# Pooled attention into a sine MLP: batch 1's q turned on VectorE, and one more inner product per unit

## The chip, the cores and the metric

The kernel runs on one core of a Trainium2 chip. Its time is device time in microseconds (us) of one launch; the kernel before has a median of 899.21 us over 3 runs (898.9 to 899.62). The profile is one execution taken by the hardware profiler; its span leaves out what lies around the program's work, so it is a little shorter than the time of a run. The engines are TensorE (PE in the profile; PEld is its weight load), VectorE (DVE), ScalarE (ACT), GpSimd (POOL) and SyncE (SP), which issues most of the DMAs.

## The reference

```python
# q, k, v: (8 batches, 8 heads, 576 rows, 64), float32
k_p = k.reshape(B, H, 72, 8, D).mean(axis=3)
v_p = v.reshape(B, H, 72, 8, D).mean(axis=3)
scores = scale * np.matmul(q, k_p.transpose(0, 1, 3, 2))
scores = scores - np.max(scores, axis=-1, keepdims=True)
attn = np.exp(scores)
attn = attn / (np.sum(attn, axis=-1, keepdims=True) + 1e-09)
out = np.matmul(attn, v_p)                       # then x: (4608 tokens, 512)
h = x @ w_in                                     # w_in: 512 x 2048
s = np.sin(alpha * h)
g = h + s * s / (alpha + 1e-09)
return g @ w_out                                 # w_out: 2048 x 512
```

Keys and values are averaged over runs of 8 rows, so each query sees only 72 of them.

## The kernel before

Everything is float32. The attention of one batch gives 576 tokens; the first matmul of the MLP goes over the 4608 tokens in 9 *units* of 512. Units 0 to 8 fill the first 517 us or so; then comes the second matmul (line L1383) to the end.

**A unit.** The first matmul is cut in halves three ways (features of x, columns of w_in, tokens) and done as seven products in place of eight, from sums of blocks (a Strassen-Winograd scheme). `hidden` runs a unit as 4 groups J of 7 *slots*, so 28 slots a unit. A slot has about one product of the group: 4 matmuls of 128x256, each recorded as 2 instructions (line L866). A group's products go to four PSUM banks `b1`, `b6`, `b5`, `b7`; ScalarE copies one bank into another so that a product adds onto it (L839), `p5` is ScalarE's copy of the fifth product to SBUF, VectorE adds `p5` to banks (L838), ScalarE takes sines (L1028) and squares (L1035), VectorE adds the squares (L1080, one add of 128x512 from PSUM and one of 128x1024 from SBUF per group) in `finish`, and `store_g` sends the result to DRAM. The tail of a group's work runs beside the first slots of the next: in the code `Q` is the group before and `G` the present one.

**The inner form.** `inner_product` does one product again as seven smaller ones: 7 matmuls of 128x128 (L1058) in place of 4 of 128x256, in four pieces `a`, `b`, `d`, `e`, between which ScalarE makes three copies (L1062, L1064, L1068) and VectorE one add (L1073). It needs sums of blocks of w_in, which GpSimd makes once in `inner_w_in` (L823), and of x, made per unit in `inner_x`. For units 1 to 6 the fifth product of groups 2 and 3 and the first of group 3 have this form (`I5 = (2, 3)`, `I1 = (3,)`).

**The attention beside it.** `carry(u)` hangs the attention of batch u + 1 on the slots of unit u by hand: a list of calls per slot, issued in that order to each engine's queue. For one batch: `load_k` and `load_v` bring k and v to SBUF, GpSimd pools them (L132), TensorE turns the pooled k (`k_t`, L279) and makes the scores in two halves (`two_scores`, L318), VectorE takes maxima and differences (`two_shifts`, L341 and L342), ScalarE the exponentials (`exp`, L367), VectorE sums and reciprocals (`norm`, L373 and L374), GpSimd multiplies (L375), VectorE turns 32x32 blocks (`turn`, L504), DMAs move them (`move`) and TensorE makes the outputs (`all_values`). Sine and exponential use different function tables of ScalarE, so a group of exps has a table load ahead of it and the next sine has another.

**q, in two ways.** The scores need q with its 64 features along the partitions. For batches 2 to 7 `turn_q` does that in two steps: VectorE transposes 32x32 blocks (L229 twice, L234 once) into `tr`, and 16 DMAs on SP's queue (L244) put the blocks in place. For batches 0 and 1 TensorE does it: for batch 1, `pairs_q` makes ScalarE put the heads in pairs (5 copies, L98), `q_t` makes 20 transposes on TensorE (L290) into PSUM in 5 steps, and each step has a copy back to SBUF (L291, two on VectorE, three on ScalarE). `columns` gives the layout of the scores' operand, which differs between the two ways.

**Queues.** Each engine runs its own list in order. DMAs issued on SP go out in order, about 0.6 us for each issue of q's moves, over eight semaphores taken in turn, so an issue waits for the one eight before it.

Of the kernel before, what the change touches and what calls it, by code (L numbers as in the profile page):

```python
# [19 lines left out]
P = 128  # L20
# [20 lines left out]
class Kernel:  # L41
# [46 lines left out]
    def pairs_q(self, b, tiles):  # L88

        nc = self.nc  # L90
        if 0 in tiles:
            self.raw = self.q_views(self.qm[b])
            self.qm[b] = self.q_tile(1)
        x = self.qm[b][:].rearrange("p (t h e d) -> p t e h d", t=5, e=2, d=self.D)
        for t in tiles:
            n = P if t < 4 else 64
            raw = self.raw[0][:, :, t, :] if t < 4 else self.raw[1]
            nc.scalar.copy(out=x[:n, t], in_=raw.rearrange("p (e h) d -> p e h d", e=2))  # L98

    def load_q_rest(self, b, at=None):  # L100
        if b < 2:
            self.nc.sync.dma_start(out=self.q_views(self.qm[b])[1] if at is None else at, in_=self.q[b, :, 4 * P:, :].rearrange("h p d -> p h d"))
# [31 lines left out]
    def load_v(self, b):  # L134

        nc, D, H = self.nc, self.D, self.H
        vm, vz = self.vp[b] = self.ap.tile([P, H // 2, D], F32, name="vm", bufs=2), self.ap.tile([P, H // 2, D], F32, name="vz", bufs=2)
        t = self.kvp.tile([P, 2048], F32, name="kvin")[:].rearrange("p (h x) -> p h x", h=4)
        x = self.kvp.tile([P, POOL * D], F32, name="vr", bufs=1)[:]
        for s in range(2):  # L140
            nc.sync.dma_start(out=t[64 * s:64 * s + 64],
                              in_=self.v[b, 4 * s:4 * s + 4, 0:4 * P, :].rearrange("h (p t) d -> p h (t d)", t=POOL))
# [5 lines left out]
        self.pool_rows(t, vm[:])  # L148
# [66 lines left out]

    def turn_q(self, b, part):
# [42 lines left out]
    def attention(self, b):  # L259
# [22 lines left out]
        def q_t(i, copy=nc.scalar.copy):  # L282

            n = rows[i]
            x = self.qm[b][:n].rearrange("p (t hp x) -> p t hp x", t=5, hp=NP)[:, i]
            if b not in self.qt:
                self.qt[b] = self.qt_view(self.q_tile(0))
            ps = self.abank([P, NP, P])
            for hp in range(NP):
                nc.tensor.transpose(ps[:, hp, :n], x[:, hp], self.ident[:n, :n])  # L290
            copy(out=self.qt_tiles(b)[:, i, :, :n], in_=ps[:, :, :n])  # L291

        def columns(hp, i):

            if b < 2:
# [230 lines left out]
        def to_x(ps, hp, t0, m, s0=0):  # L526

            while s0 < m:
# [5 lines left out]
                if t0 and b > 1:  # L534
# [8 lines left out]
        def value_parts(hp, rest):  # L543
# [14 lines left out]
            order = lambda x: x.rearrange("p a (t i) -> p t a i", i=32) if b == 1 else x  # L558
            at = lambda r, n, h: order(self.aM[r:r + n, :, 128 * h:128 * h + 128])
# [74 lines left out]
        return SimpleNamespace(**{f.__name__: f for f in (k_t, q_t, products, score, two_scores, two_shifts, exp, norm, new_a, turn, move, values, values_rest, all_values,  # L634
# [200 lines left out]
    def hidden(self, u, extra):  # L835
# [41 lines left out]
        for slot in range(7 * self.NJ):  # L877
# [9 lines left out]
            if k == 0:  # L887
# [4 lines left out]
                if G.i5 and not N:  # L892
                    G.i5.a()
                if Q and not G.i5 and not end(J):
# [5 lines left out]
                else:  # L900
                    product(G, 1, G.b1, True)
                    if G.i5:
                        product(Q, 4, Q.b7, part=(2, 3))
            elif k == 1:
                if not G.i1:
                    copy(G.b6[:], G.b1[:])
                if G.i5 and not G.i1:
# [9 lines left out]
            elif k == 2:  # L917
                if Q and not G.i5 and not split(J):
                    self.finish(Q)
                if not G.i1:  # L920
                    extras()
                if G.i1:
# [16 lines left out]
            elif k == 3:  # L939
                late = J == 0 and busy  # L940
                if Q and not late and not G.i5 and not split(J):
# [11 lines left out]
                else:  # L953
                    copy(G.b7[:], G.b6[:])
                    if G.i5:
# [10 lines left out]
                    product(G, 2, G.b1)  # L966
            elif k == 4:
# [5 lines left out]
                if not G.i5:  # L973
# [6 lines left out]
                if G.i5:  # L980
# [19 lines left out]
            else:  # L1000
# [3 lines left out]
                sin(G, 1, 1, G.g[:, 1, :, 1])  # L1004
# [19 lines left out]
    def sin(self, G, i, j, src):  # L1024

        for jj in range(JW):
# [78 lines left out]
    def first_batch(self):  # L1105
# [88 lines left out]
        self.load_w_in_part(0, ((2, 1, 0),))  # L1194
        for e in range(2):
            self.load_k(1, e)
            self.pool_k[e]()
        self.combine_w_in(0, (3,), nc.gpsimd)
# [3 lines left out]
    def carry(self, u):  # L1202
# [6 lines left out]
        if u == 0:  # L1209
# [7 lines left out]
            at(2, self.sums_of_x, 0, 3)  # L1217
# [9 lines left out]
            at(7, lambda: self.pool_v())  # L1227
# [3 lines left out]
            for i in range(2, 5):  # L1231
                at((8, 8, 9)[i - 2], A.q_t, i)
            at(9, A0.exp, 4)
            at(13, A0.norm_rest)
# [4 lines left out]
            at(8, self.combine_w_in, 2, (0, 1, 2, 3), self.nc.gpsimd)  # L1239
            at(17, self.combine_w_in, 3, (0, 1), self.nc.gpsimd)  # L1240
            at(17, self.combine_w_in, 3, (2, 3), self.nc.gpsimd)
            at(21, A0.a_rest)
            at(24.5, lambda: A0.values_rest((5, 6, 7, (self.turn + 1) % 5)))
            for r in (32, 96):
                at(3, self.nc.gpsimd.memset, self.aM[r:r + 32, :, 704:736], 0.0)
# [3 lines left out]
            at(9, self.load_q, 2)  # L1249
            at(23, lambda: self.inner_w_in(((5, 2, 4), (1, 3, 4)), (lambda w: [w[:, i * 2 * P:i * 2 * P + 2 * P] for i in range(8)])(self.q_tile(0))))  # L1250
# [3 lines left out]
            at(27, self.att[2].k_t)  # L1254
            turn = 23
# [3 lines left out]
        if 0 < u < last:  # L1259
# [453 lines left out]
```

## Time and profile before

| what | value |
|---|---|
| median of 3 runs | 899.21 us (898.9 to 899.62) |
| span of the profiled execution | 896.2 us |
| matmuls of the inner form, L1058, one group | 72 records, mean 275 ns |
| L866, 128x256, the largest group | 1072 records, mean 381 ns |
| ScalarE's exps, L367 | 29, 19.8 us |
| table loads of ScalarE at L367 and L1028 | 8 and 9, 1283 ns each |
| GpSimd's multiplies of the exps, L375 | 28, mean 1270 ns |
| DMA queue of the hardware, q1 | 137.39 MB, 52.6% of 16 engines' span |

Lines of the profile name the code line, the engine, the operation, output and input, and a count; then the busy time with the mean of one, and the idle time ahead of them. In a timeline the first number is the start in us from the span's start, the second the time that the run of like instructions takes. TensorE's matmuls overlap, so the distance from one start to the next says what one costs.

### The profile page before, as it was taken

What the parts mean: (1) busy time and instruction counts of PE and PEld (TensorE: products, weight loads), DVE (VectorE), ACT (ScalarE), POOL (GpSimd) and SP (SyncE); (2) the same over time, 40 slices, a digit from 0 to 9 for tenths busy, and PEclk for the clock granted to TensorE, in tenths of its full rate; (3) what the DMA queues carried; (4) which work ended last, traced back from release to release, by engine and by line L of the source; (5) the groups of instructions that cost most, each with busy time, mean ns of one, the idle gap of its engine ahead of it and who ended that gap; (6) DMA issues with size and microseconds to landing.
All of it is one profiled execution on the core that took longest, in us unless ns stands there. A gap on an engine that the chain in (4) does not pass through costs nothing.

```text
span 896.2 us, 16276 instructions
## 1 busy us (share of the span) xinstructions
PE 890.8 (99%) x6274; PEld 813.9 (91%) x6274; DVE 682.9 (76%) x918; ACT 438.6 (49%) x1033; POOL 249.2 (28%) x265
## 2 busy tenths in 40 slices
PE   9999999999999999999999999999999999999998
PEld 6787888888888888888888999999999999999998
DVE  7786857768577675765677889898897896996885
ACT  6687776877768777687776711111111211111111
POOL 6798443825338252434523000000000000000000
PEclk9999999999999999999999999999999999999999
DMA  9857957759586585648126243716435355164002
GB/s 269 244 158 206 244 147 212 187 164 254 139 214 186 183 225 147 175 140 302 53 106 219 102 181 103 232 37 218 117 105 160 89 159 159 37 192 142 20 18 53
DMA packets 119533, 141.03 MB, mean 157 GB/s; under 512 B 45776, under 2 KB 86496, under 8 KB 119456
## 3 DMA queue, kind: packets, MB, share of 16 engines
q1 hardware_dynamic: 116288, 137.39, 52.6%
q10 hardware_dynamic: 3168, 2.61, 1.0%
q8 instruction: 50, 0.82, 0.4%
q14 instruction: 27, 0.22, 0.1%
HBM read 75.37 MB, written 47.19 MB: 137 GB/s over the span
## 4 chain that ended last, share of the span: by engine, by line
PE 99%; DVE 0%; POOL 0%; ACT 0%; issue 0%; DVEq 0%
PE PS L866 44%; PE PS L1383 43%; PE PS L1058 5%; PE PS L318 2%; PE PS L613 2%; PE PS L626 1%; PE PS L1126 0%; PE PS L571 0%; PE PS L290 0%; PE PS L425 0%; PE PS L279 0%; PE PS L479 0%; PE PS L569 0%; POOL tr L451 0%; PE PS L403 0%; PE PS L487 0%
## 5 line engine op out<-in xcount | busy, mean ns | idle before, releaser
L866 PE MATMUL PS<-home,a 128*128 128x256 f32 x1072 | 253.0, 381 | 0.1
L866 PEld LDWEIGHTS PS<-home,a 128*128 128x128 f32 x1072 | 198.4, 190 | 30.9 <-issue 4.6
L866 PE MATMUL PS<-home,as 128*128 128x256 f32 x736 | 177.2, 382 | 0.0
L866 PEld LDWEIGHTS PS<-home,as 128*128 128x128 f32 x736 | 134.5, 190 | 18.1 <-ACT PS L839 1.2
L1383 PE MATMUL PS<-s,wb 128*128 128x192 f32 x672 | 116.2, 326 | 0.0
L1035 ACT ACTIVATE s<-s,c 128x256 f32<-128x256 f32 (+1 forms) x236 | 115.5, 556 | 0.0
L1383 PEld LDWEIGHTS PS<-s,wb 128*128 128x128 f32 x672 | 110.4, 190 | 0.1
L132 POOL TENSOR_TENSOR kvin<-kvin 96x768 f32<-96x768 f32 (+3 forms) x42 | 73.4, 1747 | 69.9 <-DMA kvin<-in_v_dram 67.8
L838 DVE TENSOR_TENSOR h<-PS,p 128x512 f32<-128x512 f32 x72 | 49.2, 684 | 55.5 <-PE PS L866 35.2
L1554 ACT COPY PS<-PS 128x192 f32<-128x192 f32 x42 | 12.7, 303 | 146.2 <-PE PS L1383 130.0
L1028 ACT ACTIVATE s<-h,al 128x256 f32<-128x256 f32 x144 | 65.5, 509 | 32.6 <-DVE h L838 32.6
L1383 PE MATMUL PS<-r,wb 128*128 128x192 f32 x432 | 79.0, 326 | 0.0
L1383 PEld LDWEIGHTS PS<-r,wb 128*128 128x128 f32 x432 | 71.6, 190 | 0.0
L1383 PE MATMUL PS<-s,a 128*128 128x192 f32 x384 | 70.2, 326 | 0.0
L1028 ACT ACTIVATE s<-PS,al 128x256 f32<-128x256 f32 x144 | 60.0, 469 | 17.2 <-PE PS L866 16.5
L1383 PEld LDWEIGHTS PS<-s,a 128*128 128x128 f32 x384 | 63.7, 190 | 0.0
L1080 DVE TENSOR_TENSOR h<-PS,s 128x512 f32<-128x512 f32 x36 | 24.8, 689 | 48.6 <-ACT s L1035 48.6
L839 ACT COPY PS<-PS 128x512 f32<-128x512 f32 x72 | 41.5, 577 | 34.5 <-PE PS L866 26.7
L1080 DVE TENSOR_TENSOR h<-h,s 128x1024 f32<-128x1024 f32 x36 | 55.3, 1537 | 3.3 <-ACT s L1035 3.1
L1584 ACT COPY PS<-PS 128x192 f32<-128x192 f32 x42 | 12.7, 303 | 89.5 <-PE PS L1383 89.5
L1322 DVE TENSOR_TENSOR s<-r 128x768 f32<-128x768 f32 x54 | 51.4, 951 | 4.8 <-PE PS L1383 2.8
L1383 PE MATMUL PS<-s,we 128*128 128x192 f32 x288 | 52.7, 326 | 0.0
(244 smaller groups left out, 1401.4 us busy)
## 6 DMA issues: line engine op xcount, KB each, us to landing
g_bridge<-h SPq DMA_DIRECT2D x72, 512.0 KB
r<-g_bridge SPq DMA_DIRECT2D x15, 1536.0 KB
x<-g_bridge SPq DMA_DIRECT2D x8, 1536.0 KB
out_dram<-o SPq DMA_DIRECT2D x90, 96.0 KB
kvin<-in_k_dram SPq DMA_DIRECT2D x14, 576.0 KB
q<-in_q_dram SPq DMA_DIRECT2D x7, 1024.0 KB
kvin<-in_v_dram SPq DMA_DIRECT2D x14, 512.0 KB
aM<-tr SPq DMA_DIRECT2D x54, 92.0 KB
```

The lines of the kernel that those rows point to most:

```text
L132: self.nc.gpsimd.tensor_tensor(out=t[..., 0:w] if w > D else out, in0=t[..., 0:w], in1=t[..., w:2 * w], op=OP.add)
L318: nc.tensor.matmul(ps[e][r0 + r:r0 + r + q.shape[-1], h, :], q[s], kb[s, hp, :], start=True, stop=True)
L613: nc.tensor.matmul(o[r:r + 64], w, x, start=start and i < 2, stop=False, skip_group_check=True)
L838: add = lambda o, x, y: nc.vector.tensor_tensor(out=o, in0=x, in1=y, op=OP.add)
L839: copy = lambda o, x: nc.scalar.copy(out=o, in_=x)
L866: nc.tensor.matmul(ps[:, jj, :], self.A[p][:, kk, f * P:(f + 1) * P], x[:, kk, :], start=(start and n == 0), stop=(kk == 1), skip_group_ch ...
L1028: self.nc.scalar.activation(out=G.s[:, i, jj, j, :], in_=src[:, jj], func=AF.Sin, scale=self.al[:, f:f + 1])
L1035: self.nc.scalar.activation(out=x, in_=x, func=AF.Square, scale=self.c[:, f:f + 1])
L1058: nc.tensor.matmul(o, W[m][:, G.J - J0], X[m], start=start and n == 0, stop=True, skip_group_check=True)
L1080: add = lambda o, x, y: self.nc.vector.tensor_tensor(out=o, in0=x, in1=y, op=OP.add)
L1322: tt = lambda o, x, y, op: nc.vector.tensor_tensor(out=o, in0=x, in1=y, op=op)
L1383: nc.tensor.matmul(out, W[:, J // 2, J % 2, :], A[:, J, :], start=(start and J == 0), stop=(J == self.NJ - 1), skip_group_check=True)
```

## The change

1. Batch 1's q is loaded raw and turned as that of batches 2 to 7 are: `pairs_q` and `q_t` go; `turn_first_q` makes three VectorE transposes and 16 DMAs on SP's queue. The last 64 rows of q are loaded in two DMAs where one did before. The batch then has the same layout as the later ones.
2. `load_v` is cut in parts: the two DMAs of the main halves, and the rest. GpSimd's pooling of the main part is a call of its own.
3. In unit 0 the work of batch 1 is hung on other slots: the moves of q stand in SP's queue with the main halves of v and w_in's part 3 between and behind them; the score halves go from slots 6 and 11 to 10 and 12; k's turn from slot 4 to 6; exps, norms and turns follow. GpSimd's sums of w_in stand at slots 4, 6, 10.5 and 16, and, ahead of unit 0, those of part 0 stand before k's pooling.
4. In units 1 to 6 the fifth product of group 1 takes the inner form too. The group's slots are re-ordered (`fast`): two halves of products are put a slot later or cut to make room, the copy `p5` comes behind the exps of slot 10, and the group's last sine goes to the next group. GpSimd's sums for the inner form are 128x384 wide in place of 128x256.
5. In these units the exps go in two pairs, at slots 6 and 10 in place of 8, 9, 10 and 10, with a one-element sine (`sine_table`) behind the first pair, so that the sine table is loaded there. Norms go to slots 7, 7, 10, 12 and turns to 9, 13, 13, 13. The main halves of v for the batch after are loaded at slot 21 of the unit before, pooled at slot 5; the rest of v stays at slot 6 (loads) and 12 (pooling).

```diff
+    def turn_first_q(self, part):
+        nc = self.nc
+        if part == 0:
+            self.tr = self.new_tr()
+            self.qt[1] = self.q_tile(1)[:]
+        tr = self.tr[:, 0:2560].rearrange("p (k x) -> p k x", k=2)
+        if part < 2:
+            x = self.q_views(self.qm[1])[0][:, 4 * part:4 * part + 4].rearrange("p hp t (k i) -> p (hp t) k i", i=32)
+            nc.vector.transpose(out=tr[:, :, 768 * part:768 * part + 512].rearrange("p k (n i) -> p n k i", i=32), in_=x)
+            return
...
+        for e, a in (((0, 1), (0, 2), (0, 3)), ((1, 0), (0, 0), (1, 1)), ((1, 2), (1, 3)))[part - 3]:
+            w = 768 if a == e else 512
+            to, at = (512, 512) if a == e == 1 else (self.q_at(a), 768 * e)
+            for k in range(2):
+                r = 64 * e + 32 * k
+                nc.sync.dma_start(out=self.qt[1][r:r + 32, to:to + w], in_=tr[32 * a:32 * a + 32, k, at:at + w])
...
-        I5, I1 = ((2, 3), (3,)) if busy else {7: ((2, 3), (2, 3)), 8: ((2, 3), (2, 3))}.get(u, ((), ()))
+        I5, I1 = ((1, 2, 3), (3,)) if busy else {7: ((2, 3), (2, 3)), 8: ((2, 3), (2, 3))}.get(u, ((), ()))
+        fast = lambda G: busy and G.J == 1
...
+                if fast(G):
+                    sin(Q, 0, 1, Q.g[:, 0, :, 1], (1,))
+                    G.i5.b()
+                    square(Q, 0, 1)
+                    product(Q, 4, Q.b7, part=(2, 3))
+                    self.last_sines(Q, 1)
+                    squares(Q, 1)
...
+                if fast(G):
+                    product(G, 6, G.b6, part=(0, 1))
+                    G.i5.d()
+                    self.finish(Q)
...
+                    if fast(G):
+                        product(G, 2, G.b1, part=(0, 1))
+                        G.i5.e()
...
                     extras()
-                    product(G, 2, G.b1)
+                    if fast(G):
+                        copy(G.p5[:], G.b5[:])
+                    product(G, 2, G.b1, part=(2, 3) if fast(G) else range(4))
...
-                sin(G, 1, 1, G.g[:, 1, :, 1])
+                if not fast(G):
+                    sin(G, 1, 1, G.g[:, 1, :, 1])
...
+    def sine_table(self):
+        self.nc.scalar.activation(out=self.sm.tile([P, 1], F32, name="order")[:], in_=self.al[:, 0:1], func=AF.Sin)
...
             for i in range(4):
-                at((8, 9, 10, 10)[i], A.exp, i)
-                at((9, 10, 11, 12)[i], A.norm, i)
-                at((12, 13, 13, 13)[i], A.turn, i)
+                at((6,6,10,10)[i], A.exp, i)
+                at((7,7,10,12)[i], A.norm, i)
+            for i in range(4):
+                at((9,13,13,13)[i], A.turn, i)
+            at(6, self.sine_table)
             at(14, A.move, range(4))
-            at(6, self.load_v, b)
+            at(5, lambda: self.pool_v_main())
+            if b < last:
+                at(21, self.load_v, b + 1, (0, 1))
+            at(6, self.load_v, b, (2,))
             at(12, lambda: self.pool_v())
```

Unit 0's list in `carry`, as far as batch 1's q, k, v and scores go:

```diff
-            at(2, self.load_w_in_part, 3)
-            at(2, self.pairs_q, 1, (0, 1))
-            at(3, self.pairs_q, 1, (2, 3, 4))
-            at(4, A.q_t, 0, self.nc.vector.tensor_copy)
-            at(4, A.q_t, 1, self.nc.vector.tensor_copy)
-            at(4, A.k_t)
-            at(7, self.load_v, 1)
+            at(3, self.turn_first_q, 0)
+            at(3, self.turn_first_q, 3)
+            for part in (1, 2, 4):
+                at(5, self.turn_first_q, part)
+            at(5, self.load_v, 1, (0,))
+            at(5, self.turn_first_q, 5)
+            at(5, self.load_v, 1, (1,))
+            at(5, self.load_w_in_part, 3)
+            at(10, self.load_v, 1, (2,))
+            at(6, A.k_t)
             for i in range(2):
-                at((6, 11)[i], A.two_scores, i)
+                at((10, 12)[i], A.two_scores, i)
...
-            for i in range(4):
-                at((9, 9, 15, 15)[i], A.exp, i)
-                at((10, 10, 16, 16)[i], A.norm, i)
-                at((13, 13, 19, 19)[i], A.turn, i)
+            for i in range(4):
+                at((12, 12, 15, 15)[i], A.exp, i)
+                at((13, 13, 16, 16)[i], A.norm, i)
+                at((15, 15, 19, 19)[i], A.turn, i)
```

More of the change, by code (lines that the diff above doesn't have):

```diff
@@ L86, in load_q_heads @@
                                in_=self.q[b, h0:h1, 0:4 * P, :].rearrange("h (p t) d -> p h (t d)", t=4))
[L88 to L98, printed above, removed]
     def load_q_rest(self, b, at=None):
-        if b < 2:
-            self.nc.sync.dma_start(out=self.q_views(self.qm[b])[1] if at is None else at, in_=self.q[b, :, 4 * P:, :].rearrange("h p d -> p h d"))
+        if b == 0:
+            self.nc.sync.dma_start(out=at, in_=self.q[b, :, 4 * P:, :].rearrange("h p d -> p h d"))
             return
@@ L280, in k_t @@
             nc.vector.tensor_copy(out=kb[:].rearrange("p hp (x j) -> p j hp x", j=3), in_=ps.rearrange("p j (hp x) -> p j hp x", hp=NP))
[L282 to L291, printed above, removed]
         def columns(hp, i):
-            if b < 2:
+            if b == 0:
                 if i == 4:
@@ L632, in all_values @@
             to_x(rest, slice(0, 4), 512, 64)
-        return SimpleNamespace(**{f.__name__: f for f in (k_t, q_t, products, score, two_scores, two_shifts, exp, norm, new_a, turn, move, values, values_rest, all_values,
+        return SimpleNamespace(**{f.__name__: f for f in (k_t, products, score, two_scores, two_shifts, exp, norm, new_a, turn, move, values, values_rest, all_values,
                                                           k_head, k_last, q_head, rest_q, products_head, soft_shift, soft_exp, norm_head, norm_rest, a_head, a_rest)})
@@ L901, in hidden @@
                     product(G, 1, G.b1, True)
-                    if G.i5:
+                    if G.i5 and not fast(G):
                         product(Q, 4, Q.b7, part=(2, 3))
@@ L906, in hidden @@
                     copy(G.b6[:], G.b1[:])
-                if G.i5 and not G.i1:
+                if fast(G):
[5 more added lines that the diff above has]
+                    squares(Q, 1)
+                elif G.i5 and not G.i1:
+                    if fast(Q):
+                        sin(Q, 1, 1, Q.g[:, 1, :, 1])
                     self.last_sines(Q, 0)
@@ L940, in hidden @@
                 late = J == 0 and busy
-                if Q and not late and not G.i5 and not split(J):
+                if Q and not late and (not G.i5 or fast(G)) and not split(J):
                     self.store_g(Q)
@@ L972, in hidden @@
                     sin(G, 0, 0, G.b1)
-                if not G.i5:
+                if not G.i5 or fast(G):
                     square(G, 0, 0)
@@ L979, in hidden @@
                 product(G, 7, G.b7, part=(0, 1))
-                if G.i5:
+                if G.i5 and not fast(G):
                     if not G.i1:
@@ L1022, in hidden, with sin @@
                     product(G, 4, G.b7, part=(3,))
-    def sin(self, G, i, j, src):
-        for jj in range(JW):
+    def sin(self, G, i, j, src, cols=range(JW)):
+        for jj in cols:
             f = i * self.K2 // 2 + G.J * JW + jj
```

64 lines of the change are left out of this document (38 added, 26 removed).

## The prediction

> **What bounds the kernel now.** I read the page first, for the engine that sets the end.
>
> ```profile
> span 896.2 us, 16276 instructions
> PE 890.8 (99%) x6274; PEld 813.9 (91%) x6274; DVE 682.9 (76%) x918; ACT 438.6 (49%) x1033; POOL 249.2 (28%) x265
> PEclk9999999999999999999999999999999999999999
> PE 99%; DVE 0%; POOL 0%; ACT 0%; issue 0%; DVEq 0%
> ```
>
> TensorE is busy 99% of the span, its granted clock is full in every slice, and the chain that ended last is TensorE for 99%. So a TensorE instruction that goes is time gained, and any wait that stops TensorE is time lost one for one; work on the other engines is free until TensorE waits for it. Then the costliest groups, for the price of each kind:
>
> ```profile
> L1058 PE MATMUL PS<-home,as 128*128 128x128 f32 x72 | 13.9, 275 | 0.0
> L290 PE MATMUL PS<-ident,q 128*128 128x128 f32 (+1 forms) x20 | 2.6, 266 | 0.0
> L98 ACT COPY q<-q 128x512 f32<-128x512 f32 (+1 forms) x5 | 2.8, 627 | 0.0
> L229 DVE STREAM_TRANSPOSE tr<-q 128x1024 f32<-128x1024 f32 x12 | 14.8, 1236 | 0.6 <-issue 0.3 <-DMA aM<-tr 0.2
> L234 DVE STREAM_TRANSPOSE tr<-q 64x512 f32<-64x512 f32 x6 | 4.0, 662 | 0.0
> L1073 DVE TENSOR_TENSOR PS<-PS,m 128x256 f32<-128x256 f32 x18 | 7.8, 432 | 23.8 <-PE PS L1058 23.8
> L367 ACT ACT_TABLE_LOAD x8 | 10.3, 1283 | 0.1
> ```
>
> A mean of 275 ns is no price of a matmul, since matmuls overlap. TensorE's timeline gives the price as a distance between starts. First unit 0, where batch 1's q is turned:
>
> ```profile
> 30.96 1.04 PE L290 MATMUL PS<-ident,q 128*128 128x128 f32 x8
> 31.84 0.41 PE L279 MATMUL PS<-ident,kp 96*128 96x96 f32 x3
> ...
> 40.38 1.06 PE L290 MATMUL PS<-ident,q 128*128 128x128 f32 x8
> 41.28 1.89 PE L866 MATMUL PS<-home,as 128*128 128x256 f32 x8
> 43.10 0.46 PE L290 MATMUL PS<-ident,q 64*128 64x64 f32 x4
> 43.49 1.99 PE L866 MATMUL PS<-home,as 128*128 128x256 f32 x8
> 45.32 1.89 PE L866 MATMUL PS<-home,a 128*128 128x256 f32 x8
> ```
>
> Then unit 2, with a plain stretch and the start of an inner product:
>
> ```profile
> 207.42 3.62 PE L866 MATMUL PS<-home,a 128*128 128x256 f32 x16
> 210.87 3.62 PE L866 MATMUL PS<-home,as 128*128 128x256 f32 x16
> ...
> 220.41 0.39 PE L1058 MATMUL PS<-home,as 128*128 128x128 f32 x2
> 220.63 0.39 PE L1058 MATMUL PS<-last,q 128*128 128x128 f32 x2
> ```
>
> 16 records of 128x256 take 210.87 − 207.42 = 3.45 us, 0.216 each, and one product (4 matmuls, 8 records) 1.73. Two records of 128x128 take 0.22, so 0.111 each.
>
> **The change, part by part.**
>
> *Batch 1's q.* The 20 transposes go. First eight: 31.84 − 30.96 = 0.88. From 40.38 to 45.32 TensorE spends 4.94 on twelve transposes and two products; two products are 3.46, so 1.48. The k transposes (L279) lose their neighbour of like shape: behind a 128x256 product their first took 382 ns instead of 216 elsewhere in the trace (81.35 us), so 0.17 comes back. 0.88 + 1.48 − 0.17 = **−2.2 us**. With them go five ScalarE copies (L98, 2.8 us) and five evictions (L291), off the path, so worth nothing.
>
> Added are three VectorE transposes, by L229 and L234 2 × 1.24 + 0.66 = 3.1 us, 16 DMAs on SP's queue for the moves (L244's twin), and one more for the load of the tail in two halves: 17. The first two score products are put from slots 6 and 11 to 10 and 12, and must find the moved q. In before's time frame: batch 1's q lands at 28.2 (issued 13.7), VectorE can turn it at about 29.9 to 31.2, and SP, which issues such a move in 0.59 us (median of 96), puts twelve out from 31.2 to 38.2. Moves of this kind land 2.0 to 2.2 us after issue in a quiet queue, 2.5 to 4.4 in a busy one, so the last of the twelve at 40.3 to 42.6. TensorE reaches the scores near 41.9. Reckoned at 2.2 it waits for nothing; at 4.4 it waits 0.7. Queued behind those moves on SP's queue are w_in's part 3 and v's main halves, which feed GpSimd's pooling, the normalised rows, their moves and the value products at slot 26: I get the last of those moves down at 73.4 and the value products at 74.15, cover 0.7. GpSimd's queue changes too: w_in's last sums of part 0 go ahead of the k pooling, which then ends at 32.3, before the k transposes near 34.6. I allow 0.1 for unit 0.
>
> *The inner form, units 1 to 6.* A product of 8 × 0.216 = 1.73 becomes 14 records of 128x128, 7 matmuls: 14 × 0.111 = 1.55. That is 0.18 saved, six times: **−1.05 us**. Per unit it adds three ScalarE copies and one VectorE add (0.43, L1073). GpSimd's four sums per unit for w_in take 128x384 in place of 128x256, in its idle time.
>
> *The exps in two pairs.* Each unit now has four table loads instead of two, 2 × 1.28 us more of ScalarE, plus a dummy sine. ScalarE is idle half the span, but not in this group:
>
> ```profile
> 212.90 1.28 ACT L367 ACT_TABLE_LOAD   x1
> 214.20 1.26 ACT L367 ACTIVATE ex<-ex 128x576 f32<-128x576 f32 x2
> ...
> 217.86 1.28 ACT L1028 ACT_TABLE_LOAD   x1
> ```
>
> The order in which ScalarE now goes through the second group, from the sine at 205.02, with distances between starts from the timeline: two sines 0.41 each, a table load and two exps to 208.5, a load and the dummy to 209.95, two copies of the inner product (0.30, 0.27), sine, copy, sine, copy (0.41, 0.49, 0.41, 0.16) to 212.0, two squares (0.80), two sines from PSUM (0.73), two wide squares (1.24), the copy to b7 (0.49) to 215.3, a third load 1.30, exps of 0.59 and 0.92, and the copy to p5, whose end falls at 218.55 to 218.75. VectorE's add on it (0.69, L838) ends 219.25 to 219.45, and product 4 of this group, which writes the same bank, is due at 219.55 − 0.17 = 219.38. So TensorE waits between 0 and 0.1 us; the waits' own delays put me at the upper end: 6 × 0.1 = **+0.6 us**. Behind product 4 on TensorE is everything. The copies for the inner product itself have cover of 0.15 to 0.6 (210.3 against 210.45, 212.0 against 212.6, 215.3 against 215.9). Moved work that I cost at nothing: this group's last sine goes to the third group's ScalarE idle time (0.74 us at 222.8), so that group's copy to b6 ends at 223.1 where TensorE needs it at 223.2; without that cover it costs up to one sine pair, 0.8 a unit. The turns and the moves of the rows start 0.4 us later, at 225.2, with 1.9 us to spare at the value products. v's main halves are loaded a group or more earlier, two issues of 0.64 us on SP ahead of q's moves; GpSimd sat 10.57 us for them at 211.3, so its pooling now ends near 206.
>
> The Trainium skill, in "ScalarE: Activation LUTs", section "What ACT_TABLE_LOAD costs", adds a drain of about 1380 ns to a load of about 1283 ns. By it three loads ahead of p5 would delay that copy by another 4.1 us. The trace has the load at 1283 ns, but with 18 ns before it and 12 ns behind it, so the sum goes without a drain.
>
> VectorE has the wide add of L1080 at 215.4 to 216.6 ahead of that p5 add, then a turn and a reduction; done by 218.3. Where GpSimd pools beside it the same add took 1.64 to 2.17 us (3.00 once) instead of 1.17 to 1.23 alone.
>
> The Trainium skill, "SBUF — State Buffer", section "Who interferes with whom", has VectorE with two SBUF inputs contend with GpSimd for whole instructions; these rows agree.
>
> **Sum** against the profiled 896.2: −2.2 − 1.05 + 0.6 + 0.1 = −2.55, so a span near 893.65. The median of the runs is 899.21, 3.0 above the span for what lies around it: 896.7.
>
> **Rivals.**
>
> *A. ScalarE's chain is later than reckoned.* Thirteen back-to-back microseconds leave no cover; with 0.4 us late per unit (as long as one sine) it is 6 × 0.4 = 2.4 instead of 0.6: 898.5. For it: nothing absorbs lateness. Against: every duration is from the trace.
>
> *B. The wide add meets GpSimd's multiplies.* Reckoned, those end about 213.9 and the add starts at 215.4. If GpSimd is more than 1.5 us later, the add takes up to 0.95 more, VectorE reaches the p5 add at 219.2 and TensorE waits 0.6 per unit: 3.6 instead of 0.6, 899.7.
>
> *C. Slower: the moves of batch 1's q come late.* They share SP's queue with w_in, v and k of batch 2, and the trace has landings up to 8 us after issue when that queue is full (the 16 engines are nearly all busy from 2.5 to 40 us). The last needed piece, issued at 38.2, then lands at 46.2; TensorE waits 4.3 at the first scores: −2.55 − 0.1 + 4.3 = +1.65, 900.9. It is a loss from a landing after 44.5 on. Against: what they move falls from some 350 GB/s at 33 us to 28 at 43.
>
> *D. The drain counts after all.* 4.1 − 0.1 per unit, 6 × 4 = 24 us: 920. The rows around every load deny it.
>
> *E. The change doesn't do what it says,* or less: new small waits eat the gain, 899.2.
>
> **How the numbers follow.** Forecast 896.7, chance 0.60; A 0.14, B 0.08, C 0.11, D 0.01, E 0.06. A measurement of this kernel can tell about 0.2%, 1.8 us, from no change. Faster than 897.4: the forecast with most of its own spread, and the mild end of A: 0.66. Slower than 901.0: D, half of C, and stalls that add up: 0.11. The rest, 0.23, is within. The low end, 895.5, has no stalls at all (−3.25) and 0.45 for a gain elsewhere; the high end, 900.6, takes in A, B, E and part of C. The forecast's own range is 895.8 to 897.4.
>
> **What would show it.** In unit 0: no L290 rows, and no gap on TensorE before the first scores (a gap released by a DMA is C) or before the value products. In units 1 to 6: 84 more records of 128x128, 448 in all; 29 table loads for exps and sines instead of 17, with no gap around them; TensorE's gap ahead of the second group's product 4 near 0.1 us (0.4 is A), and the wide add in that group at 1.2 us (2 is B). The prediction is wrong if TensorE's idle time grows by more than 1.5 us, or if ScalarE's chain shows a wait that I have as covered.

## The result

The changed kernel takes 900.69 us (median of 21 runs, 899.24 to 902.4) against 899.14 for the kernel before (21 runs); the ratio is 1.002, with a 95% interval of 1.0014 to 1.0026. It is slower by 1.5 us where 2.5 us faster were forecast. A second set of runs of the same kernel (again, below) gave a ratio of 1.0007 (0.9998 to 1.0016). By the two ratios the loss is 1.8 and 0.6 us, and the second interval takes in no change; a gain of 2.5 us lies outside both.

The page of the profile after (of the slowest of the 21 runs, 902.40 us), with the lines that answer to those shown of before:

```profile
span 900.6 us, 16396 instructions
PE 890.7 (99%) x6290; PEld 814.1 (90%) x6290; DVE 684.3 (76%) x925; ACT 454.9 (51%) x1061; POOL 245.1 (27%) x265
PEclk9999999999999999999999999999999999999999
PE 93%; POOL 2%; DMA 2%; ACT 1%; SPq 1%; issue 1%; DVE 0%; ACTq 0%; POOLq 0%; DVEq 0%
```

Before, TensorE was 99% of the chain that ended last; now 7% of the span belongs to others: GpSimd, the DMAs, ScalarE and SP's queue. TensorE is busy as long as before (890.7 against 890.8 us) in a span that is 4.4 us longer: it waits more. The view of TensorE's waits between 20 and 110 us, which was empty before, gives what it waited for (us in total, times, the longest):

```profile
PE PS L615 <- DMA aM<-tr: 1.7, 1, 1.7
PE PS L869 <- DVE h L840: 1.4, 2, 1.0
PE PS L321 <- DMA q<-tr: 0.5, 1, 0.5
```

The timeline of TensorE puts them in place; the bracket is the idle time before the line, and what ended it:

```profile
65.67 1.99 PE L869 MATMUL PS<-home,a 128*128 128x256 f32 x8 [0.96 <-DVE h L840]
70.44 3.72 PE L869 MATMUL PS<-home,as 128*128 128x256 f32 x16 [0.40 <-DVE h L840]
80.30 0.65 PE L615 MATMUL PS<-aM,vm 64*64 64x512 f32 x6 [1.72 <-DMA aM<-tr]
99.60 1.00 PE L321 MATMUL PS<-kblk,q 64*64 64x72 f32 x46 [0.52 <-DMA q<-tr]
```

Three are in unit 0, one in unit 1: two on a VectorE add, one on the moves of the normalised rows (`aM<-tr`) ahead of the value products, one on batch 2's q. Of these places the prediction had looked at the value products alone, and gave them 0.7 us of cover.

What is late first is seen on GpSimd (unit 0), first before:

```profile
42.79 4.56 POOL L132 TENSOR_TENSOR kvin<-kvin 128x1024 f32<-128x1024 f32 x2 [4.85 <-DMA kvin<-in_v_dram]
...
55.47 2.25 POOL L375 TENSOR_TENSOR ex<-ex,sm 128x576 f32<-128x576 f32 x2
```

Then the changed kernel:

```profile
52.16 3.71 POOL L120 TENSOR_TENSOR kvin<-kvin 128x1024 f32<-128x1024 f32 x2 [5.78 <-DMA kvin<-in_v_dram]
55.95 0.73 POOL L120 TENSOR_TENSOR vm<-kvin 128x256 f32<-128x256 f32 x1
56.63 1.27 POOL L690 TENSOR_TENSOR as<-a,a 128x512 f32<-128x512 f32 x1
57.98 1.27 POOL L690 TENSOR_TENSOR as<-as,a 128x512 f32<-128x512 f32 x1
59.21 2.25 POOL L378 TENSOR_TENSOR ex<-ex,sm 128x576 f32<-128x576 f32 x2
```

GpSimd sat 5.78 us for v, pooled it, made two sums of w_in, and only then came the multiplies of the exps at 59.21. Counted from unit 0's first product (19.07 before, 21.71 now), they are 1.1 us later than before, while TensorE, rid of the transposes, comes some 2 us earlier to what depends on them. VectorE's next instruction waits for them, and behind it in VectorE's queue stands the add that TensorE needs at 65.67:

```profile
60.39 0.71 DVE L507 STREAM_TRANSPOSE tr<-ex 128x512 f32<-128x512 f32 x1 [1.78 <-POOL ex L378]
...
64.93 0.68 DVE L840 TENSOR_TENSOR h<-PS,p 128x512 f32<-128x512 f32 x1
```

SP's queue shows why the row moves are late. First before, then after:

```profile
43.63 0.38 SPq L85 DMA_DIRECT2D q<-in_q_dram  x1
...
65.52 7.88 SPq L524 DMA_DIRECT2D aM<-tr  x12
```

```profile
57.58 0.39 SPq L85 DMA_DIRECT2D q<-in_q_dram  x1
59.82 2.42 SPq L94 DMA_DIRECT2D q<-in_q_dram  x2
67.71 10.88 SPq L527 DMA_DIRECT2D aM<-tr  x12
```

Twelve row moves took 7.88 us to issue before and 10.88 now. An issue waits for the DMA eight before it, and those were now the loads of k and q for batch 2, which the trace has landing at 64.4 to 71.1 us: the second of the twelve went out at 70.61, when a load of q had landed at 70.59. Before, all loads had landed by 57.2. The last row move lands at 80.16 (before 74.92). The DMA engines' share in slices of 1.5 us from 20 to 80 us, before and then after, says the same:

```profile
DMA  9999999999999520399999950000000897658999
```

```profile
DMA  9999999993444435399999999999999357525656
```

Before, the engines had a free stretch of seven slices (56 to 66 us) ahead of the row moves. After, they are only 30 to 50% busy from 33.5 to 45.5 us, while SP issues the 16 small moves one by one, and full from there to 66.5.

**By stage**, worked out from the starts in the timelines: from unit 0's first product of TensorE (L866 before, L893 in b_only, else L869) to the first of batch 1's last value products (L626, L652, else L628), and from there to the same of batch 2. The runs below the changed kernel are those of the next section:

| kernel | first product at | unit 0 | unit 1 | median, us | ratio to before (95%) |
|---|---|---|---|---|---|
| before | 19.07 | 59.60 | 53.53 | 899.14 | |
| changed | 21.71 | 61.15 | 54.20 | 900.69 | 1.0014 to 1.0026 |
| changed, again | 19.71 | 60.63 | 54.29 | 899.87 | 0.9998 to 1.0016 |
| a_only | 19.71 | 60.14 | 54.63 | 901.29 | 1.0019 to 1.0038 |
| b_only | 19.81 | 59.49 | 53.43 | 897.65 | 0.9981 to 0.9999 |
| v_first | 19.78 | 59.41 | 54.11 | 899.41 | 1.0003 to 1.0021 |
| pool_late | 20.06 | 62.94 | 53.65 | 902.25 | 1.0023 to 1.0045 |
| q2_late | 19.95 | 58.10 | 59.24 | 902.93 | 1.0037 to 1.0061 |
| v_act | 21.50 | 60.84 | 53.94 | 901.57 | 1.0015 to 1.0035 |
| v_act_swap | 19.71 | 61.10 | 54.03 | 900.97 | 1.0015 to 1.0033 |
| q2_swap | | | | 899.83 | 0.9997 to 1.0015 |
| sums_later | 21.66 | 58.89 | 54.85 | 899.75 | 0.9995 to 1.0012 |
| sums_later_v2 | 19.53 | 62.21 | 53.17 | 901.62 | 1.0017 to 1.0036 |
| both_late | 19.31 | 57.46 | 53.16 | 896.33 | 0.9960 to 0.9983 |

The profiled execution of q2_swap ran at a granted clock of 0.949, so its stages are left out.

The span of the changed kernel is 4.4 us longer than before's, yet the median only 1.5. Unit 0 has 1.55 of it and unit 1 0.67; units 2 to 6 give back 0.63 in all; and 2.64 is the start-up, which differs between executions of one program: 21.71 in one profile of the changed kernel, 19.71 in the other. Without the start-up the stages come to +1.6 in the first profile and +1.1 in the second, near what the medians say.

### The profile page after: what moved, and what is told of

The parts are those of the page before. It is cut to its first block, busy times and chain, and to the rows that moved or that the text cites. A ratio compares the mean times of both kernels' runs of the same rounds, so it can differ in the third digit from the quotient of the medians.

```text
span 900.6 us, 16396 instructions
## 1 busy us (share of the span) xinstructions
PE 890.7 (99%) x6290; PEld 814.1 (90%) x6290; DVE 684.3 (76%) x925; ACT 454.9 (51%) x1061; POOL 245.1 (27%) x265
## 4 chain that ended last, share of the span: by engine, by line
PE 93%; POOL 2%; DMA 2%; ACT 1%; SPq 1%; issue 1%; DVE 0%; ACTq 0%; POOLq 0%; DVEq 0%
PE PS L1420 42%; PE PS L869 39%; PE PS L1087 6%; PE PS L321 2%; PE PS L615 2%; DMA g_bridge<-h 1%; PE PS L628 1%; POOL kvin L120 1%; SPq L258 1%; DMA q<-in_q_dram 1%; POOL ex L378 0%; ACT s L1054 0%; DMA q<-tr 0%; ACT L370 0%; ACT ex L370 0%
## 5 line engine op out<-in xcount | busy, mean ns | idle before, releaser
L869 PE MATMUL PS<-home,a 128*128 128x256 f32 x1072 | 255.4, 381 | 1.1 <-DVE h L840 1.0
L869 PEld LDWEIGHTS PS<-home,a 128*128 128x128 f32 x1072 | 197.1, 190 | 30.9 <-issue 4.6
L869 PE MATMUL PS<-home,as 128*128 128x256 f32 x688 | 167.8, 382 | 0.4 <-DVE h L840 0.4
L869 PEld LDWEIGHTS PS<-home,as 128*128 128x128 f32 x688 | 124.9, 190 | 17.3 <-ACT PS L841 1.2
L120 POOL TENSOR_TENSOR kvin<-kvin 96x768 f32<-96x768 f32 (+3 forms) x42 | 70.4, 1677 | 8.0 <-DMA kvin<-in_v_dram 5.8
L378 POOL TENSOR_TENSOR ex<-ex,sm 128x576 f32<-128x576 f32 (+1 forms) x28 | 35.3, 1270 | 73.6 <-DVE sm L377 39.4
L1109 DVE TENSOR_TENSOR h<-h,s 128x1024 f32<-128x1024 f32 x36 | 51.8, 1439 | 3.3 <-ACT s L1061 3.1
```

What stands on the lines that cost most here:

```text
L120: self.nc.gpsimd.tensor_tensor(out=t[..., 0:w] if w > D else out, in0=t[..., 0:w], in1=t[..., w:2 * w], op=OP.add)
L378: nc.gpsimd.tensor_tensor(out=E(i), in0=E(i), in1=sm.unsqueeze(2).to_broadcast([P, n, Sp]), op=OP.mult)
L869: nc.tensor.matmul(ps[:, jj, :], self.A[p][:, kk, f * P:(f + 1) * P], x[:, kk, :], start=(start and n == 0), stop=(kk == 1), skip_group_ch ...
L1109: add = lambda o, x, y: self.nc.vector.tensor_tensor(out=o, in0=x, in1=y, op=OP.add)
```

## The experiments

All start from the changed kernel, with the edits shown, and have its line numbers (b_only's are 24 higher in the lines named here). Each is compared with runs of the kernel before made beside it.

**One part at a time: a_only.**

```diff
-        I5, I1 = ((1, 2, 3), (3,)) if busy else ...
+        I5, I1 = ((2, 3), (3,)) if busy else ...
...
-        fast = lambda G: busy and G.J == 1
+        fast = lambda G: False
...
-                at((6,6,10,10)[i], A.exp, i)
+                at((8, 9, 10, 10)[i], A.exp, i)
...
-            at(6, self.sine_table)
```

> The change of batch 1's q and unit 0 alone: group 1's fifth product stays plain in units 1 to 6 and their exps, norms and turns stay in the old slots. Theory V (in unit 0 v's main halves land late behind q's moves, GpSimd pools them ahead of the multiplies of the exps, and TensorE waits about 4 us in unit 0 and at the start of unit 1; the inner form itself gains about 1): slower than the changed kernel by about 1.0, so 901.5 to 902, with the waits of TensorE near 64, 70, 78 and 99 us still there. Theory S (ScalarE's chain in units 1 to 6 is what costs): faster than before, near 897. Theory H (the start-up, up to the first product of unit 0, is about 2.5 us later for good): the first products stand 2.5 us later than before in this profile too.

901.29 us, 2.5 above the 898.75 of before beside it. Its profile has the four waits at the same places (0.48, 0.41, 1.30 and 0.55 us) and one more of 0.22 at batch 2's scores, with the first product at 19.71.

**b_only**: the kernel before's unit 0, `pairs_q` and `q_t` put back, with the changed kernel's `hidden` and its slots of units 1 to 6.

> The inner form and the slots of units 1 to 6 alone, with batch 1's q turned on TensorE and unit 0 as before. Theory V: 0.17 us a unit gained, 1.0 in all, so 898.1 with no new wait on TensorE. Theory S: slower than before, 900 or more. Theory H says nothing other than V here.

897.65 us against 898.75: 1.1 faster, with no wait on TensorE between 20 and 112 us. The two parts add up: +2.5 − 1.1 = +1.4, near the +1.5 of the whole change. Theory S falls, and so does H: a_only's start-up is at 19.71, and b_only's, which is the kernel before's, at 19.81.

**v_first.**

```diff
-            at(5, self.load_v, 1, (0,))
-            at(5, self.turn_first_q, 5)
-            at(5, self.load_v, 1, (1,))
+            at(5, self.load_v, 1, (0, 1))
+            at(5, self.turn_first_q, 5)
```

> The changed kernel with both main halves of v ahead of q's last four moves in SP's queue. Theory V: the second half is issued some 2.5 us earlier, GpSimd's pooling starts 2 to 3 us earlier, and TensorE's waits near 65, 70 and 78 us shrink by 2 to 3 us in all; the last four moves land later and the second half of the scores may wait up to 1.5 us: 898 to 899.5. Theories S and H: as the changed kernel, 900.7, or slower by the wait at the scores.

899.41 us, inside the range. The waits on VectorE and on the row moves are gone, and the wait is at the second half of the scores instead, whose q moves now land behind v (TensorE's timeline of this run):

```profile
49.40 1.51 PE L321 MATMUL PS<-kblk,q 64*64 64x72 f32 x78 [1.95 <-DMA q<-tr]
95.85 1.00 PE L321 MATMUL PS<-kblk,q 64*64 64x72 f32 x46 [0.63 <-DMA q<-tr]
```

**pool_late.**

```diff
-            self.vin = self.kvp.tile([P, 2048], F32, name="kvin")[:].rearrange(...)
+            self.vin = (self.q_tile(0)[:, 0:2048] if b == 1 else self.kvp.tile(...)[:]).rearrange(...)
...
-            at(10, lambda: self.pool_v_main())
...
+            at(17, lambda: self.pool_v_main())
```

> The changed kernel with v's main halves of batch 1 loaded into the tile that held raw q, and their pooling on GpSimd put behind the multiplies of the exps (slot 17 instead of 10). The landing of v is as late as in the changed kernel. Theory V: the first multiply starts about 2 us earlier, the four waits of TensorE (1.1, 0.6, 1.9 and 0.7 us) are gone or below 0.5 in all, and the time is 896 to 897. If the lateness of the exps alone (slot 12 instead of 9) were the cause, the waits stay and the time with them, 900.7. Theory H: not below 899.

902.25 us: a miss by 5 us. The first half of the expectation held: the multiplies start at 55.40 in place of 59.21; 1.65 us of that is an earlier start-up, and 2.2 are left; and the waits on VectorE's add are gone. But the row moves, ready earlier, met the loads (SP's queue, then TensorE):

```profile
58.05 2.29 SPq L94 DMA_DIRECT2D q<-in_q_dram  x2
64.95 12.32 SPq L527 DMA_DIRECT2D aM<-tr  x12
```

```profile
78.96 1.12 PE L615 MATMUL PS<-aM,vm 64*64 64x512 f32 x6 [3.90 <-DMA aM<-tr]
```

The twelve issues now take 12.32 us: the second was held from 65.52 to 69.09, until batch 2's q had landed at 69.07. So late pooling is one cost, and the loads still on their way at 65 to 71 us are another; theory V had only the first. It was widened to V2: the 16 moves in SP's queue push every load behind them later.

**q2_late**: pool_late with one more edit.

```diff
-            at(13, self.load_q, 2)
+            at(20, self.load_q, 2)
```

> The kernel with late pooling of v, with batch 2's q loaded behind the row moves (slot 20 instead of 13). There TensorE waited 3.9 us for the row moves, which waited for semaphores held by loads that landed at 69 to 70 us. Theory V2: with 1.15 MB less in the queue the loads end near 65, the row moves go out without a break, and that wait is gone or below 1; the lateness shows instead in the transposes of batch 2's q, which wait for it, and in the scores of unit 1. Sum uncertain, 898 to 903. If the row moves were late for another cause (their own turns), the 3.9 us stay.

With 1.15 MB out of the queue the row moves were issued from 64.90 to 73.1 and the value products had no wait; unit 0 is 4.8 us shorter than in pool_late (62.94 − 58.10). The price came on VectorE, as expected, but it stopped TensorE at a product of unit 1 and not at the scores:

```profile
82.04 2.37 DVE L243 STREAM_TRANSPOSE tr<-q 128x1024 f32<-128x1024 f32 x2 [7.99 <-DMA q<-in_q_dram]
```

```profile
85.62 5.24 PE L869 MATMUL PS<-home,a 128*128 128x256 f32 x16 [3.57 <-DVE h L840]
```

**v_act, q2_swap, v_act_swap.** The first issues v's main halves on ScalarE's queue:

```diff
+            at(4, self.load_v, 1, (0, 1), nc.scalar)
...
-            at(5, self.load_v, 1, (0,))
...
-            at(5, self.load_v, 1, (1,))
```

> The changed kernel with both main halves of v issued on ScalarE's queue at slot 4, while SP issues q's moves; nothing else moved. Theory V2 (the new moves of q fill SP's queue and its eight semaphores, so every load behind them is some 10 us later: v is then late for GpSimd, and the loads of k and q for batch 2 still land when the normalised rows are to be moved): GpSimd pools v before the exps are ready, the waits of TensorE near 64 and 70 us are gone, the loads end 2 to 4 us earlier, and the wait at the value products falls from 1.9 below 1: 897 to 898. Rival L (only the eight semaphores pace the row moves): the wait at the value products stays near 2 to 4 us, as in the run with late pooling, and the time is 899 to 901.

901.57 us, a miss, and rival L was no better: the value products had no wait at all, so it came to its time by another way. v was pooled at 46.1 and the loads ended at 68.4, but the moves of q, which share the DMA engines with v, landed 4 to 7 us after issue in place of 2, and the first half of the scores waited 1.74 us. The Trainium skill, "DMA: Bandwidth & Descriptors", section "Rules for kernel authors", says that spreading DMAs over issuing engines gives no bandwidth, since all run on the same 16 DMA engines; this run agrees. What the wait cost beyond its length stands at the end of this document.

The second exchanges the q tiles, since batch 1's turned q had taken the tile that batch 2's q was loaded into:

```diff
-        self.qm[b] = self.q_tile(b > 1)
+        self.qm[b] = self.q_tile(0)
...
-            at(13, self.load_q, 2)
+            at(9, self.load_q, 2)
-            at(23, lambda: self.inner_w_in(..., (...)(self.q_tile(0))))
+            at(23, lambda: self.inner_w_in(..., (...)(self.q_tile(1))))
```

> The changed kernel with the two q tiles exchanged from batch 2 on (batch 2's q goes where batch 1's raw q was, the weights of the inner form into the other), so that batch 2's q need not wait for batch 1's scores and is loaded at slot 9 instead of 13. Theory V2: the same bytes in another order, v as late as before, so the waits near 64 and 70 stay; q of batch 2 lands earlier and k later; the wait at the value products changes little or falls by up to 1: 900 to 901. A rival, that the place of batch 2's q load is the whole cause: the wait at the value products is gone, 898.5.

899.83 us, between before's 899.04 and the changed kernel's 900.69. The third has both edits:

> Both of the two edits (v on ScalarE's queue, the q tiles exchanged and batch 2's q at slot 9). Theory V2: no wait on TensorE over 0.5 us in unit 0; near 896.5 to 897.5. If it is no better than the one with v on ScalarE's queue alone, the place of batch 2's q does not count.

900.97 us, a miss: q's moves still met v, and the scores waited 1.9 us.

**sums_later** (the exchange of tiles, and `combine_w_in(3, (0, 1))` at 13.5 in place of 10.5) **and sums_later_v2** (that, and `load_v(2, (0, 1))` on ScalarE's queue at slot 24).

> The changed kernel with two edits in unit 0: the q tiles exchanged so that batch 2's q loads at slot 9, and on GpSimd the sums of w_in of slot 10.5 put behind the first two multiplies of the exps (13.5). Theory V2 with both of its costs met: the multiplies start as soon as the exps are summed (the waits near 64 and 70 us below 0.3 in all), the loads end near 65 us so the row moves go out without a break, and the wait at the value products is below 0.5. What is left is the wait at batch 2's scores in unit 1, below 1: 896.5 to 898. If the loads on the queue as a whole are too much for unit 0 in any order, a wait of 2 us or more turns up at another place and the time is 899 or more.

> The same, with batch 2's main halves of v issued on ScalarE's queue (slot 24 instead of 22), so that SP issues batch 2's q moves 1.3 to 2 us earlier: the wait at batch 2's scores in unit 1 (0.7 to 1 us) is gone and the time is 0.5 to 1 below the run before it, unless ScalarE's own queue holds up a copy of unit 0's end.

899.75 and 901.62 us, both misses. In the first the value products had no wait: the loads had landed by 67.5 and the row moves went out in a row. But the w_in sums, now between the two pairs of multiplies, made the second pair late, and TensorE waited 1.37 us for VectorE's add; batch 2's scores waited 0.44 and 0.73. In the second the wait of unit 1 was gone, as expected, but one of 2.98 us turned up at the value products. Its cause is in the trace: ScalarE's queue issued the first 512 KB of v just before SP issued the last of the row moves, at 73.64:

```profile
73.26 0.72 ACTq L131 DMA_DIRECT2D kvin<-in_v_dram  x1
```

```profile
79.29 0.65 PE L615 MATMUL PS<-aM,vm 64*64 64x512 f32 x6 [2.98 <-issue]
```

The load landed at 78.79 and the move behind it at 79.09, 5.4 us after its issue; the move before it, issued at 73.01 ahead of the load, landed at 75.14.

**The changed kernel again.**

> The changed kernel itself once more, on the same chip as these two. If the late start-up of its profile (first product at 21.7 us against 19.1) belongs to the change, it is there again; if it varies between executions, the first product stands near 20, and the waits of unit 0 sum to 3 to 4 us as before. 900.7 either way.

Its waits of 0.92, 0.41, 1.26 and 0.70 us stand where the first profile had 0.96, 0.40, 1.72 and 0.52.

**both_late**: an edit for each of the three waits.

```diff
-        self.qm[b] = self.q_tile(b > 1)
+        self.qm[b] = self.q_tile(0)
...
-            at(10.5, self.combine_w_in, 3, (0, 1), self.nc.gpsimd)
+            at(16, self.combine_w_in, 3, (0, 1), self.nc.gpsimd)
...
-            at(13, self.load_q, 2)
+            at(9, self.load_q, 2)
...
-            at(22, self.load_v, 2, (0, 1))
+            at(27, self.load_v, 2, (0, 1))
```

> The changed kernel with three edits: the q tiles exchanged so that batch 2's q loads at slot 9; GpSimd's sums of w_in of slot 10.5 put behind all four multiplies of the exps (slot 16); batch 2's main halves of v loaded behind the moves of batch 2's q (slot 27 instead of 22). Theory V2: each of the three waits of the changed kernel has its cause met: no wait near 64 and 70 us, none at the value products, none over 0.3 at batch 2's scores, so TensorE keeps the 2.2 us of unit 0 and the 1.0 of units 1 to 6: 896 to 897. If a wait of 1 us or more is left in unit 0 or 1, the queue has no order with room for the 16 moves among those tried, and the time is 898 or more.

896.33 us against 898.52 for the kernel before beside it, ratio 0.9972 (0.9960 to 0.9983): 2.2 us faster than before, where the changed kernel was 0.6 to 1.8 slower. The view of TensorE's waits from 20 to 112 us is empty again. GpSimd's multiplies start when the exps are summed, and the sums of w_in come behind the second pair. v is pooled no sooner than in the changed kernel (30.7 us after the first product, 30.5 there), so here it was the sums in between that held the multiplies up; sums_later, with v as late, has its first multiply 35.4 us after the first product, both_late 35.3, the changed kernel 37.5:

```profile
53.75 0.73 POOL L120 TENSOR_TENSOR vm<-kvin 128x256 f32<-128x256 f32 x1
54.65 2.26 POOL L378 TENSOR_TENSOR ex<-ex,sm 128x576 f32<-128x576 f32 x2 [0.17 <-DVE sm L377]
...
59.14 2.83 POOL L378 TENSOR_TENSOR ex<-ex,sm 128x576 f32<-128x576 f32 x2 [0.84 <-DVE sm L377]
61.92 1.28 POOL L690 TENSOR_TENSOR as<-a,a 128x512 f32<-128x512 f32 x1
```

On SP's queue the row moves take 8.82 us, and the moves of batch 2's q 11.11 where the changed kernel took 14.06, with v's loads behind them:

```profile
63.43 8.82 SPq L527 DMA_DIRECT2D aM<-tr  x12
72.35 3.27 SPq L1123 DMA_DIRECT2D g_bridge<-h  x4
76.94 11.11 SPq L258 DMA_DIRECT2D q<-tr  x16
88.15 1.36 SPq L131 DMA_DIRECT2D kvin<-in_v_dram  x2
```

Of the three edits the first was run by itself (q2_swap), and with other places for the sums (sums_later); what the other two are worth by themselves was not tried.

## Why the prediction was wrong

**The gain on TensorE was right.** The 20 transposes less the dearer k turn were put at 2.2 us: where nothing waits (both_late) unit 0 is 59.60 − 57.46 = 2.14 us shorter. The inner form was put at 0.18 a unit and 1.05 in all: like units go from 55.07 to 54.90 us between value products, and b_only measured 1.1. (The kernel before has one longer interval among units 2 to 6, 55.25, and the changed kernel two, 55.09, so that its five units give back 0.63 and not 0.85; why stays open.)

**ScalarE's chain was right to 0.25 us, and its stall of +0.6 mis-sized: it was 0.** In unit 2 of the changed kernel, ScalarE, VectorE and TensorE:

```profile
222.82 0.57 ACT L841 COPY p<-PS 128x512 f32<-128x512 f32 x1
```

```profile
220.27 1.21 DVE L1109 TENSOR_TENSOR h<-h,s 128x1024 f32<-128x1024 f32 x1
...
223.42 0.69 DVE L840 TENSOR_TENSOR h<-PS,p 128x512 f32<-128x512 f32 x1 [0.25 <-ACT p L841]
```

```profile
222.54 1.89 PE L869 MATMUL PS<-home,as 128*128 128x256 f32 x8
224.27 1.03 PE L869 MATMUL PS<-home,a 128*128 128x256 f32 x4
```

This unit runs 4.88 us later than in the trace before (209.90 against 205.02 for the sine), so the copy to p5 ends at 218.51 in before's frame, where 218.55 to 218.75 was reckoned, and the add at 219.23. Product 4 starts at 222.54 + 1.73 = 224.27: no wait, and TensorE has none in units 2 to 6. Rival A did not happen. Neither did B, the wide add takes 1.21 us, nor D: every load takes 1.28 us and no drain is seen. E's time is near, but the change did all that it says.

**The step that failed is "I get the last of those moves down at 73.4 and the value products at 74.15, cover 0.7", and with it "I allow 0.1 for unit 0."** The row moves landed at 80.16, 77.5 with the later start-up taken off: 4.1 us later. Counted from start to start, as the price of a matmul is, the three waits cost 1.1, 0.6 and 1.8 us, and the value products take 0.2 longer than before: 3.7 us in unit 0 where 0.1 stood in the sum. The sign of being wrong that the prediction named, over 1.5 us more idle time on TensorE, is there: 3.6 us between 20 and 110. Two things were not put in time. The moves of q were followed to their landing, and they were on time (no wait at batch 1's scores). But the loads behind them are named and have no landing of their own: v's second half was issued at 45.94 and landed at 52.09, and GpSimd has its pooling ahead of the multiplies. And the prediction did not speak of the load of batch 2's q, moved from slot 9 to 13 because its tile now holds batch 1's turned q; the trace has it landing at 70.6 to 71.1 instead of 49.0 to 50.6, in the way of the row moves. pool_late and q2_late show the two one after the other. The trace before already had v's loads landing 8.6 and 9.3 us after issue.

**A second, smaller step: v's loads "ahead of q's moves" at no cost.** The two DMAs of batch 2's v stand ahead of the moves of its q, and unit 1's scores wait 0.52 to 0.70 us; with the loads on ScalarE's queue (sums_later_v2) or behind the moves (both_late) the wait is gone. But b_only has the same two loads ahead of the same moves and no wait, so the order by itself is not the cost. In the changed kernel unit 0 is shorter on TensorE and the row moves ahead are later; which of these takes the cover away was not tried.

**Rival C named the right queue and the wrong wait.** It had q's moves late at the first scores, and lost 4.3 us there. They were not late; the loads that they displaced were. The loss is of the same size, 3.2 to 3.7 us in unit 0 if both_late's 57.46 is taken as what is possible (against 60.63 and 61.15), and 1.0 to 1.1 in unit 1 (53.16 against 54.20 and 54.29), so that −3.2 in both_late's stages became +1.1 to +1.6. That C's time, 900.9, lies so near the measured one is luck.

## What to carry to other kernels

Where transfers move into a queue that is already full, what they cost is found behind them: list every DMA that follows in that queue, put issue and landing in time, and go on to the first reader of each and what stands behind that reader on its engine. A free stretch of the DMA engines ahead of a time-critical group of small transfers is a resource; a load that drifts into it is paid twice, by its bytes (the last row move of sums_later_v2, 5.4 us in place of 2.1) and by the semaphores it holds (the second row move of pool_late, held for 3.6 us). When a change of layout gives a buffer a new owner, look for the load that now has to wait for it.

## What the runs showed of the hardware

A stop of TensorE can cost more than its length. In v_act it waited 1.74 us at the scores, and the granted clock behind it was 0.50 for a while. The view by stretches of that run (the stretch, its length, busy time and count of each engine, then the granted clock, the DMA share and GB/s):

```profile
45.80:48.00 2.20, 2.18 (x65) 1.97 (x66) 1.11 (x3) 0.00 (x0) 2.20 (x2) 0.70 0.40 96
48.00:50.00 2.00, 2.00 (x5) 1.56 (x5) 1.93 (x4) 0.00 (x0) 1.84 (x3) 0.50 0.58 175
50.00:54.00 4.00, 4.00 (x93) 3.35 (x91) 1.39 (x4) 3.06 (x6) 0.98 (x2) 0.99 0.86 303
```

Matmul records of 128x256 started 0.43 us apart there instead of 0.216. After 3.57 us of waiting in q2_late the clock was 0.50 too (16 such matmuls took 5.08 us from start to start of the next group, instead of 3.45), after 3.90 us in pool_late it averaged 0.59 over 4 us, and after 1.92 us in v_act_swap it was 0.50 from 46 to 48 us. But behind waits of 1.72 us (changed kernel), 1.95 (v_first) and 2.98 (sums_later_v2) it stayed at 1.00. So the length of a wait alone does not decide. The Trainium skill, "TensorE: Matmul & The Clock Gate", section "What's actually happening", has the clock drop after an idle window of about 3.4 us, in windows that run freely; the free running would fit the scatter, but a drop after 1.74 us is sooner than that page has it. The matmuls right behind that wait are small ones, the scores' of 64x72; whether they count as work for the clock is not shown.

The single runs show the price. Each has a mean granted clock on record. The stretches above lose about 1.7 us of full clock, 0.2% of the span (worked out from them), and v_act's profiled run has 0.998. Of v_act's twelve runs, six at 1.000 took 899.25 to 900.83 us, and six at 0.996 or 0.998 took 902.31 to 903.06. In pool_late six of seven runs are at 0.996 to 0.998, and the seventh, at 1.000, took 899.71; in q2_late all five are. So part of what these runs lost is the clock. The changed kernel has 20 of its 21 runs at 0.999 or 1.000, and those at 1.000 alone go from 899.42 to 902.40: its spread comes from something else.
